# The hand-over from attention to routed experts: other places for five row stores, a list's steps and an early read

## The chip, the cores and the metric

The kernel runs on one core of a Trainium2 chip. The metric is the device time of one execution in microseconds. Shown are the median of three timed runs and one execution under the hardware profiler, from which all rows of the trace come.

The engines are named as in the profile: PE (TensorE), DVE (VectorE), ACT (ScalarE), POOL (GpSimd) and SP (SyncE, which here only issues transfers and loads registers). A transfer issued by SP or POOL runs on the core's DMA engines.

## The reference

Block-causal attention over 8 batches of 8 heads (576 positions, head size 64), whose output, transposed to 4608 rows of 512, goes through a mixture of experts with 4 groups of 4 experts; each row goes to the best expert of its best group.

```python
def _attn_ref(q, k, v):
    scores = np.matmul(q, k.transpose(0, 1, 3, 2)) / np.sqrt(D)
    scores = np.where(block_i >= block_j, scores, -1e9)      # blocks of 64
    attn = softmax(scores)
    return np.matmul(attn, v)

def _moe_ref(x, w_group, w_expert, w1, w2):                  # x: 4608 x 512
    g_idx = np.argmax(x @ w_group, axis=1)
    for g in range(4):
        xg = x[g_idx == g]
        e_idx = np.argmax(xg @ w_expert[g], axis=1)
        for e in range(4):
            h = np.maximum(xg[e_idx == e] @ w1[g, e], 0.0)   # 512 -> 1024
            ye = h @ w2[g, e]                                # 1024 -> 512
            out[rows of e] = (g_weight * e_weight)[:, None] * ye
```

## The kernel before, in words

**Attention.** The 64 heads are worked on in 32 pairs, one `period` for each; a pair is on the way over several periods. What an engine does in a period follows a list written by hand (`ORDER`): S are the scores, D the row maxima (L214), E the exponentials (L224), T the transposes of the weights (L252) with their copies t, V the values products (L291) with their copies v into the tile `xT`. Four pairs make a batch of 576 rows, and for each batch the router's tokens run in the same list: X0, X1, ... transpose `xT` back and store the scaled rows (`xns`) to the table of rows `xd` in memory; L, n, Y, M and G0 to G4 compute the router's logits, the choice and each row's place in its expert's list (`base` counts the rows of each expert); Z0 to Z4 scatter a batch's row numbers into the lists (`tab`), by POOL.

**The early list.** When five of the eight batches are counted, the fullest expert has its first 512 rows. `early` picks it with a few small DVE instructions and writes its number and the list's start to `rowe`. It is a generator: whoever calls `next` on it gets the instructions up to the next `yield`. The loop over pairs hangs such calls behind tokens of a period (`behind`; `eb` is 19, so `eb + 8` is period 27). SP then reads `rowe` into registers (`index`), reads the list from `tab` into `idse` (`getids`, L899) and loads the expert's weights, one piece for each `ask(1)` (`rawe`, 512 KB, L937). POOL gathers the 512 rows (`xge`, L910). So the first expert's two products (`g1`, L1009, and `g2`, L1059) can begin before the last batch is routed.

**The seam.** After the loop `seam` ends the attention of the last pair, and from then on PE runs the expert's plan (`moe.run`): g1 of piece 0, 1, 2, g2 of piece 0, g1 of 3, g2 of 1, and so on in turn. After place n of this plan come the calls in `moe.hooks[n]`: the last batch's router tokens (`last` is batch 7, `before` 6, `third` 5), the row stores X0 to X4 of the last batch (four PE transposes, eight ACT scalings at L648, one store at L649), and the four steps of `final`. `final` is a generator too: on DVE it computes from the counts the plan of all other lists, and its last step stores it to `rowi` (L558). Hook 6 also reads the first planned list (`getids` of slot 1: the registers from the plan by L880 and L881, then five reads of `tab` into `ids`, L899), and hook 7 gathers its rows from `xd` (`xg`, L910, by POOL). That gather reads rows of any batch, so it waits for every row store. PE transposes the gathered rows (L968). Behind each place the plan also splits weights into a high and a low half (`whe` by ACT at L953, `wle` by DVE at L954); L1032 on DVE makes the low half of a hidden piece (`hring`, `hx`), whose high half ACT makes at L1025.

Each engine, and each queue of transfers, works through its instructions in the order in which the program issues them.

```python
for h in hooks.get(n, []):       # moe.run: behind place n of the plan
    h()
```

Of the kernel before, what the change touches and what calls it, by code (L numbers as in the profile page):

```python
# [13 lines left out]
ALU = mybir.AluOpType  # L14
# [92 lines left out]
class Attention:  # L107
# [30 lines left out]
    def one(self):  # L138
        if self.after:
            return self.psT(), None  # L140
        h = self.banks.take(0, 1)
        return self.banks.view(h.ids[0]), h
# [237 lines left out]
class Router:  # L380
# [111 lines left out]
    def early(self, row):  # L492
        one = [R, 1]
        cnt = self.tt(self.base[0:R], self.eb, ALU.subtract)
        mx = self.red(cnt, ALU.max)
        sc = self.stt(cnt, mx[:, 0:1], self.edesc, ALU.is_ge, ALU.mult)
        m2 = self.red(sc, ALU.max)
        yield
        oh = self.ts(sc, m2[:, 0:1], ALU.is_equal)
        self.stt(cnt, 512.0, oh, ALU.min, ALU.mult, out=self.taken)  # L500
        self.ts(m2[0:1], -1.0, ALU.mult, float(NE), ALU.add, out=row[0:1, 0, 0:1])
        st = self.red(self.tt(oh, self.eb, ALU.mult))
        self.nc.vector.tensor_copy(row[0:1, 0, 1:2], st[0:1])
        yield

    def final(self, row):
# [309 lines left out]
def make_consts(tc, pool):  # L816
    nc = tc.nc
    ident = pool.tile([P, P], F32, name="ident")
    make_identity(nc, ident)
    return dict(ident=ident)  # L820
# [437 lines left out]
def seam(at, ro, moe, inner, ctx, N, rowi):  # L1258
    e, last, before, third = moe.slots[0], N // 4 - 1, N // 4 - 2, N // 4 - 3
    a = lambda i, *tok: at.token(i, tok, N)  # L1260
    r = lambda b, *toks: [ro.token(at, b, (t[0], int(t[1]))) for t in toks]
    at.on_dve = SEAM_DVE
    ro.later = set()
    y, z = N - 2, N - 1

    r(before, "X2", "X0", "X1")
    moe.advance(2, 99)
    at.gated()
    moe.gather(e, 3)
    r(third, "Z0")  # L1270
    a(y, "V", 0)
    a(y, "V", 1)
    a(y, "v", 0)
    moe.advance(2, 99)
    a(y, "v", 1)
    r(before, "G0", "G1", "G2")
    for g in (1, 0, 2):
        a(z, "T", g)
        a(z, "t", g, 0)
        a(z, "t", g, 1)  # L1280
    held = [at.banks.take(0, 1), at.banks.take(0, 1), at.banks.take(1, 2)]
    hold = [(0, 0), (1, 0), (2, 0), (2, 1)]
    for c, (n, m) in enumerate(hold):
        moe.xt_turn(e, c, at.banks.view(held[n].ids[m]))
    r(last, "R0")
    r(third, "Z1", "Z2")
    a(z, "V", 0)
    a(z, "V", 1)
    for c, (n, m) in enumerate(hold):
        moe.xt_split(e, c)  # L1290
        held[n].done()
    a(z, "v", 0)
    moe.advance(2, 99)
    a(z, "v", 1)
    inner.close()
    moe.open(ctx)
    moe.grow()
    moe.ngat = moe.nxt = len(e["ch"])
    at.after = at.moe = True
    fin = ro.final(rowi)  # L1300
    step = lambda: next(fin, None)
    one = lambda *toks: [lambda t=t: r(*t) for t in toks]
    moe.hooks = {
        0: one((last, "L0", "n0", "n1", "L1", "n2", "n3"), (before, "G4", "G3"), (third, "Z3", "Z4")),
        1: one((last, "Y0", "M0", "Y1", "M1", "Y2", "M2", "G0", "G1", "G2"), (before, "Z0", "Z1")),
        2: one((last, "X0"), (before, "Z2", "Z3")),
        3: one((before, "Z4"), (last, "X1")),
        4: one((last, "G4", "G3")) + [step],
        5: one((last, "Z0", "Z1", "Z2", "X2")) + [step] * 2,
        6: one((last, "Z3", "Z4", "X3")) + [step, lambda: moe.getids(moe.slots[1])],  # L1310
        7: one((last, "X4")) + [moe.hold, lambda: moe.gathers(1e9, True)],
    }
    at.spare = [(4, 5), (6, 7), (4, 5), (6, 7), (2, 3)]
    moe.steps = moe.run(moe.hooks)


@with_exitstack
def attention_moe(ctx, tc, q, k, v, wcat, w1, w2, out, order=None, on_dve=None):
    nc = tc.nc
    order = order or ORDER  # L1320
    on_dve = ON_DVE if on_dve is None else on_dve
    N = q.shape[0]
    NBAT = N // 4
    dp = ctx.enter_context(tc.tile_pool(name="dp", bufs=1, space=bass.MemoryType.DRAM))
    tab = dp.tile([TABR, TROW], I32, name="tab")
    xd = dp.tile([NTOK + 1, 512], F32, name="xd")
    cp = ctx.enter_context(tc.tile_pool(name="cp", bufs=1))
    consts = make_consts(tc, cp)
    rowe = cp.tile([1, 1, 2], I32, name="rowe")
    rowi = cp.tile([1, R, 2], I32, name="rowi")  # L1330
    rowo = cp.tile([1, R, 2], I32, name="rowo")
    cnti = cp.tile([1, 1], I32, name="cnti")
    inner = ExitStack()
    ET = mybir.EngineType
    with tc.manual_schedule(engines={ET.PE, ET.Activation, ET.DVE, ET.Pool, ET.SP}):
        ro = Router(tc, ctx, consts, wcat, tab, xd)
        moe = Moe(tc, ctx, consts, ro, w1, w2, out)
        at = Attention(tc, ctx, inner, q, k, v, consts)
        at.router, moe.at = ro, at
        warm = cp.tile([P, 1], F32, name="warm")  # L1340
        nc.vector.memset(warm, 0.0)
        nc.scalar.activation(warm, warm, AF.Exp)
        at.start(N, on_dve)
        at.clear()
        pre = ro.setup()
        eb = 4 * EBAT - 1
        slots = [moe.slot("e", FULL, rowe, slice(0, 1))]
        slots += [moe.slot(i, CAPS[i], rowi, slice(i, i + 1)) for i in EXEC]
        moe.plan(slots)
        ear = ro.early(rowe)  # L1350
        e = slots[0]
        for x in range(N):
            behind = {}
            if 2 <= x < 8:
                step = len(order) // HK
                behind = {order[step * z + step - 1][0]: [lambda: next(pre, None)] for z in range(HK)}
            if x == eb + 2:
                behind = {("T", 0): [lambda: moe.blank(e, 0), lambda: moe.blank(e, 1)]}
            if x == eb + 3:
                behind = {("T", 0): [lambda: moe.blank(e, 2), lambda: moe.blank(e, 3)]}  # L1360
            if x == eb + 8:
                behind = {t: [lambda: next(ear, None)] for t in (("S", 0), ("V", 1), ("T", 0))}
            if x in (eb + 9, eb + 10, eb + 11):
                behind = {("V", 1): [lambda: moe.index(e), lambda: moe.ask(1)]}
            if x == eb + 10:
                behind["end"] = [lambda: moe.getids(e)]
            if x == eb + 12:
                behind = {("V", 1): [lambda: at.load_v(N - 1), lambda: moe.ask(1)]}
            ahead = [lambda c=c: (at.gated(), moe.gather(e, c)) for c in {eb + 11: (0, 1), eb + 12: (2,)}.get(x, ())]
            at.period(x, N, order, behind, ahead)  # L1370
        seam(at, ro, moe, inner, ctx, N, rowi)
        spl = ro.spill(at, rowo, cnti)
        hooks = moe.hooks
        for n in range(60, 66):
            hooks[n] = [lambda: next(spl, None)]
        for _ in moe.steps:
            pass
    moe.overflow(cnti, rowo)
# [47 lines left out]
```

## Time and profile before

| | |
|---|---|
| median of three runs | 745.92 us (744.05 to 746.36) |
| the profiled execution's own time | 742.96 us |
| its span, first to last instruction | 741.2 us |
| what lies around the span | 1.8 us |
| PE, DVE, ACT, POOL busy | 97%, 63%, 60%, 35% of the span |
| bytes moved | 129.89 MB, 175 GB/s over the span |

Busy shares are means over stages with different limits. The attention and the experts differ, and the seam between them lies at about 262 to 330 us of the span. An idle engine costs something only where what it waits for ends last.

### The profile page before, as it was taken

What the parts mean: (1) busy time and instruction counts of PE and PEld (TensorE: products, weight loads), DVE (VectorE), ACT (ScalarE), POOL (GpSimd) and SP (SyncE); (2) the same over time, 40 slices, a digit from 0 to 9 for tenths busy, and PEclk for the clock granted to TensorE, in tenths of its full rate; (3) what the DMA queues carried; (4) which work ended last, traced back from release to release, by engine and by line L of the source; (5) the groups of instructions that cost most, each with busy time, mean ns of one, the idle gap of its engine ahead of it and who ended that gap; (6) DMA issues with size and microseconds to landing.
All of it is one profiled execution on the core that took longest, in us unless ns stands there. A gap on an engine that the chain in (4) does not pass through costs nothing.

```text
span 741.2 us, 20996 instructions
## 1 busy us (share of the span) xinstructions
PE 719.5 (97%) x7944; PEld 590.6 (80%) x7944; DVE 468.6 (63%) x1166; ACT 445.5 (60%) x1204; POOL 262.9 (35%) x560
## 2 busy tenths in 40 slices
PE   7999999999999999879999999999999999999996
PEld 4777777777777777769988888888898998888894
DVE  4878889888898877524335437537566456655642
ACT  6999898999989874424334335425455445544531
POOL 5534466665755654413121402302311303103102
PEclk9999999999999999989999999999999999999999
DMA  6953536264554642363335762672667428538441
GB/s 227 370 172 132 194 90 230 85 225 142 170 193 148 216 147 66 107 246 128 107 123 198 233 252 81 204 271 95 188 214 291 145 86 292 188 114 280 153 163 44
DMA packets 51623, 129.89 MB, mean 175 GB/s; under 512 B 12646, under 2 KB 13286, under 8 KB 51520
## 3 DMA queue, kind: packets, MB, share of 16 engines
q1 hardware_dynamic: 42592, 103.94, 41.6%
q0 software_dynamic: 8928, 24.60, 9.2%
q8 instruction: 63, 1.03, 0.6%
q14 instruction: 40, 0.33, 0.1%
HBM read 104.05 MB, written 24.59 MB: 174 GB/s over the span
## 4 chain that ended last, share of the span: by engine, by line
PE 87%; DVE 3%; ACT 3%; DMA 3%; issue 2%; POOL 1%; SPq 1%; POOLq 0%; DVEq 0%; ACTq 0%
PE psum L1059 23%; PE psum L1009 23%; PE psum L291 11%; PE psum L209 10%; PE psum L252 7%; PE psum L1004 5%; PE psum L1064 2%; PE psum L968 2%; ACT pb L224 2%; PE psum L1079 2%; DMA xd<-xns 1%; PE psum L658 1%; DMA xg<-xd,ids 1%; PE psum L301 1%; DMA idse<-tab 1%
## 5 line engine op out<-in xcount | busy, mean ns | idle before, releaser
L224 ACT ACTIVATE pb<-psum,nm 128x384 f32<-128x384 f32 (+8 forms) x288 | 149.6, 543 | 22.4 <-DVE nm L214 22.2
L1009 PE MATMUL psum<-xt,wh 128*128 128x264 f32 (+6 forms) x704 | 155.4, 312 | 0.0
L214 DVE TENSOR_REDUCE nm<-psum 128x1 f32<-128x384 f32 (+8 forms) x288 | 118.7, 482 | 13.8 <-PE psum L209 13.0
L1105 POOL DMA_INDIRECT out_dram<-ys,ids x40 | 41.0, 1025 | 238.9 <-DVE ys L1101 221.1
L1009 PEld LDWEIGHTS psum<-xt,wh 128*128 128x128 f32 x704 | 118.9, 188 | 8.1 <-issue 1.7
L1009 PE MATMUL psum<-xt,wl 128*128 128x264 f32 (+6 forms) x352 | 109.2, 310 | 0.0
L1025 ACT ACTIVATE hring<-psum 128x256 fp32r<-128x256 f32 (+5 forms) x68 | 32.0, 471 | 124.6 <-PE psum L1009 55.7
L1059 PE MATMUL psum<-wh,hring 128*128 128x512 f32 x306 | 106.6, 399 | 0.0
L291 PE MATMUL psum<-pt,vb 128*64 128x64 f32 (+4 forms) x1152 | 94.1, 317 | 0.6 <-ACT pt L268 0.6
L954 DVE TENSOR_TENSOR wl<-raw,wh 128x512 fp32r<-128x512 f32 x144 | 93.1, 686 | 1.7 <-ACT wh L953 1.5
L291 PEld LDWEIGHTS psum<-pt,vb 128*64 128x64 f32 x1152 | 66.5, 137 | 34.3 <-ACT pb L224 9.2
L209 PE MATMUL psum<-natk,natq 64*64 64x128 f32 (+5 forms) x1792 | 90.5, 339 | 2.8 <-ACT pb L224 1.2
L1032 DVE SCALAR_TENSOR_TENSOR hring<-psum,hring 128x256 fp32r<-128x256 f32 (+4 forms) x91 | 37.3, 431 | 81.7 <-ACT hring L1025 81.6
L268 ACT COPY pt<-psum 128x512 f32<-128x512 f32 x159 | 81.7, 619 | 1.5 <-PE psum L252 1.5
L953 ACT CAST wh<-raw 128x512 fp32r<-128x512 f32 x144 | 82.2, 620 | 0.2
L209 PEld LDWEIGHTS psum<-natk,natq 64*64 64x64 f32 x1792 | 57.4, 133 | 26.3 <-issue 3.4
L910 POOL DMA_INDIRECT xg<-xd,ids x40 | 40.8, 1020 | 85.7 <-PE psum L968 37.7
L1009 PEld LDWEIGHTS psum<-xt,wl 128*128 128x128 f32 x352 | 66.2, 188 | 1.0
L1059 PEld LDWEIGHTS psum<-wh,hring 128*128 128x128 f32 x306 | 57.5, 188 | 11.5
L224 ACT ACTIVATION_READ_ACCUMULATOR pb<-psum,nm 128x1 f32 x288 | 62.9, 218 | 0.0
L252 PE MATMUL psum<-ident,pb 64*128 64x64 f32 x1536 | 58.9, 225 | 2.9 <-ACT pb L224 2.6
L1059 PE MATMUL psum<-wl,hring 128*128 128x512 f32 x153 | 60.2, 393 | 0.0
(217 smaller groups left out, 1122.2 us busy)
## 6 DMA issues: line engine op xcount, KB each, us to landing
raw<-in_w_dram SPq DMA_DIRECT2D x72, 512.0 KB, 4.5
vb<-in_v_dram SPq DMA_DIRECT2D x32, 384.0 KB, 4.8
natk<-in_k_dram SPq DMA_DIRECT2D x32, 288.0 KB, 4.6
natq<-in_q_dram SPq DMA_DIRECT2D x32, 288.0 KB, 5.6
wh<-in_w_dram SPq DMA_DIRECT2D x16, 512.0 KB, 4.8
xd<-xns SPq DMA_DIRECT2D x14, 512.0 KB, 2.8
keep<-in_w_dram SPq DMA_DIRECT2D x12, 512.0 KB, 4.3
kept<-in_w_dram SPq DMA_DIRECT2D x12, 512.0 KB, 7.3
```

The source lines that it names most:

```text
L209: self.gate = nc.tensor.matmul(st[bank][c:c + 64, c0:c0 + n], lhsT=q[ps, BLK * t:BLK * t + BLK], rhs=k[ps, k0:k0 + n], start=True, stop=Tr ...
L214: self.nc.vector.tensor_reduce(out=r["nm"][:, t:t + 1], in_=r["s", t], op=ALU.max, axis=AX.X if t < 8 else AX.XY, negate=True)
L224: nc.scalar.activation(reg, r.pop(("s", t)), AF.Exp, bias=r["nm"][:, t:t + 1], accum_out=self.sms[b][:, pr, t:t + 1])
L252: self.gate = self.nc.tensor.transpose(out=out[a], in_=x[ps], identity=self.c["ident"][ps, ps], tile_position=(64 * a, 0))
L268: self.nc.scalar.copy(dst, src)
L291: nc.tensor.matmul(o[64 * a:64 * a + 64, BLK * (t0 - b0):BLK * (t1 - b0)], lhsT=r["v"][:, a, j, :], rhs=r["pt"][:, PHALF * (a ^ f) + c0:PH ...
L910: self.nc.gpsimd.indirect_dma_start(out=x[0:n], out_offset=None, in_=src, in_offset=bass.IndirectOffsetOnAxis(ap=s["ids"][0:n, c, 0:1], ax ...
L953: nc.scalar.copy(h[:, sl], s["raw", u][:, sl])
L954: nc.vector.tensor_tensor(out=l[:, sl], in0=s["raw", u][:, sl], in1=h[:, sl].bitcast(F32), op=ALU.subtract)
L1009: nc.tensor.matmul(o, lhsT=ww[:, dc, f], rhs=rr[:, dc, t], start=dc == 0 and x == 0, stop=dc == 3 and x == 2)
L1059: nc.tensor.matmul(y[c][0:n], lhsT=hh, rhs=w, start=k == 0 and x == 0, stop=k == 7 and x == 2)
L1105: i = nc.gpsimd.indirect_dma_start(out=self.out, out_offset=bass.IndirectOffsetOnAxis(ap=s["ids"][0:n, c, 0:1], axis=0), in_=ys[0:n], in_o ...
```

## The change

Three edits, all in the order of work; no computation is added or left out.

1. In `early` the `yield`s stand at other places: five pieces instead of two, and the product `taken`, which only `final` reads, comes last. The pieces hang behind tokens of two pairs (`eb + 8` and `eb + 9`) instead of one.
2. The registers of the early list are read at the end of period `eb + 9` instead of behind its V1; the list itself (`idse`) is read behind V1 of period `eb + 10`, ahead of that period's weight load, instead of at the period's end.
3. In the seam's hooks X0 comes in hook 0 (was 2), X1 in 2 (was 3), X2 in 3 (was 5), X3 in 4 (was 6), X4 in 5 (was 7). The steps of `final` are two in hook 4 and two in hook 5 (were one, two and one).

```diff
         cnt = self.tt(self.base[0:R], self.eb, ALU.subtract)
         mx = self.red(cnt, ALU.max)
+        yield
         sc = self.stt(cnt, mx[:, 0:1], self.edesc, ALU.is_ge, ALU.mult)
         m2 = self.red(sc, ALU.max)
         yield
         oh = self.ts(sc, m2[:, 0:1], ALU.is_equal)
-        self.stt(cnt, 512.0, oh, ALU.min, ALU.mult, out=self.taken)
         self.ts(m2[0:1], -1.0, ALU.mult, float(NE), ALU.add, out=row[0:1, 0, 0:1])
+        yield
         st = self.red(self.tt(oh, self.eb, ALU.mult))
         self.nc.vector.tensor_copy(row[0:1, 0, 1:2], st[0:1])
+        yield
+        self.stt(cnt, 512.0, oh, ALU.min, ALU.mult, out=self.taken)
         yield
...
-        0: one((last, "L0", "n0", "n1", "L1", "n2", "n3"), (before, "G4", "G3"), (third, "Z3", "Z4")),
+        0: one((last, "L0", "n0", "n1", "L1", "n2", "n3"), (before, "G4", "G3"), (last, "X0"), (third, "Z3", "Z4")),
         1: one((last, "Y0", "M0", "Y1", "M1", "Y2", "M2", "G0", "G1", "G2"), (before, "Z0", "Z1")),
-        2: one((last, "X0"), (before, "Z2", "Z3")),
-        3: one((before, "Z4"), (last, "X1")),
-        4: one((last, "G4", "G3")) + [step],
-        5: one((last, "Z0", "Z1", "Z2", "X2")) + [step] * 2,
-        6: one((last, "Z3", "Z4", "X3")) + [step, lambda: moe.getids(moe.slots[1])],
-        7: one((last, "X4")) + [moe.hold, lambda: moe.gathers(1e9, True)],
+        2: one((last, "X1"), (before, "Z2", "Z3")),
+        3: one((before, "Z4"), (last, "X2")),
+        4: one((last, "G4", "G3")) + [step] * 2 + one((last, "X3")),
+        5: one((last, "Z0", "Z1", "Z2")) + [step] * 2 + one((last, "X4")),
+        6: one((last, "Z3", "Z4")) + [lambda: moe.getids(moe.slots[1])],
+        7: [moe.hold, lambda: moe.gathers(1e9, True)],
...
-            if x == eb + 8:
+            if x in (eb + 8, eb + 9):
                 behind = {t: [lambda: next(ear, None)] for t in (("S", 0), ("V", 1), ("T", 0))}
-            if x in (eb + 9, eb + 10, eb + 11):
-                behind = {("V", 1): [lambda: moe.index(e), lambda: moe.ask(1)]}
+            if x == eb + 9:
+                behind["end"] = [lambda: moe.index(e), lambda: moe.ask(1)]
             if x == eb + 10:
-                behind["end"] = [lambda: moe.getids(e)]
+                behind = {("V", 1): [lambda: moe.getids(e), lambda: moe.ask(1)]}
+            if x == eb + 11:
+                behind = {("V", 1): [lambda: moe.ask(1)]}
```

The built programs show the new order. First SP's queue in the seam, from the fourth row store of the last batch (`xns_3`) to the first weight load of the first planned list; before, where the last row store (`xns_4`) stands behind the five reads of the list (`ids`):

```order
L649 DMA xd<-xns_3_6247 128x512
L558 DMA rowi<-fin_6267 1x64x2
L880 TENSOR_LOAD fin_6267
L881 TENSOR_LOAD fin_6267
L899 DMA ids_6289<-tab 128x4x2
L899 DMA ids_6289<-tab 16x2
L649 DMA xd<-xns_4_6317 64x512
L937 DMA raw_0_6338<-in_w_dram 128x1024
```

In the changed program (its lines have numbers three higher) the same instructions of SP stand so:

```order
L652 DMA xd<-xns_3_6191 128x512
L561 DMA rowi<-fin_6243 1x64x2
L652 DMA xd<-xns_4_6251 64x512
L883 TENSOR_LOAD fin_6243
L884 TENSOR_LOAD fin_6243
L902 DMA ids_6303<-tab 128x4x2
L902 DMA ids_6303<-tab 16x2
L940 DMA raw_0_6338<-in_w_dram 128x1024
```

The last row store has moved ahead of the register loads and the list's reads; of these the row of 16x2 stands for four.

Second, DVE at the end of `final`, from the last instructions of its third step (`fin`) on; before:

```order
L474 TENSOR_SCALAR fin_6217<-fin_6211 64x1
L954 TENSOR_TENSOR wle_6220<-rawe_5707,whe_6219 128x512 x2
L1032 SCALAR_TENSOR_TENSOR hring<-psum,hring 128x512
L484 SCALAR_TENSOR_TENSOR fin_6257<-fin_6209,pid,fin_6201 64x16
L484 SCALAR_TENSOR_TENSOR fin_6257<-scan_439,fin_6211,fin_6213 64x16
L474 TENSOR_SCALAR vals<-fin_6215,fin_6217 64x16
L479 TENSOR_TENSOR fin_6261<-vals,fin_6257 64x96
```

And DVE in the changed program:

```order
L474 TENSOR_SCALAR fin_6231<-fin_6225 64x1
L484 SCALAR_TENSOR_TENSOR fin_6233<-fin_6223,pid,fin_6183 64x16
L484 SCALAR_TENSOR_TENSOR fin_6233<-scan_439,fin_6225,fin_6227 64x16
L474 TENSOR_SCALAR vals<-fin_6229,fin_6231 64x16
L479 TENSOR_TENSOR fin_6237<-vals,fin_6233 64x96
L489 TENSOR_REDUCE fin_6239<-fin_6237 64x3
L474 TENSOR_SCALAR fin_6241<-fin_6239 64x1
L558 CAST fin_6243<-fin_6239 64x1
L479 TENSOR_TENSOR fin_6243<-fin_6239,fin_6241 64x1
L957 TENSOR_TENSOR wle_6262<-rawe_5707,whe_6261 128x512 x2
L1035 SCALAR_TENSOR_TENSOR hring<-psum,hring 128x512
```

The two weight splits and the low half of a hidden piece stand behind the fourth step instead of ahead of it.

Third, SP in period `eb + 10`, from the last pair's queries (`natq`) on; before:

```order
L170 DMA natq_5064<-in_q_dram 128x576
L937 DMA rawe_5152<-in_w_dram 128x1024
L638 DMA xd<-xns_2_5163 64x512
L638 DMA xd<-xns_0_5221 128x2x512
L638 DMA xd<-xns_1_5257 128x2x512
L899 DMA idse<-tab 128x4x2
```

And SP in the changed program:

```order
L170 DMA natq_5064<-in_q_dram 128x576
L902 DMA idse<-tab 128x4x2
L940 DMA rawe_5154<-in_w_dram 128x1024
L641 DMA xd<-xns_2_5165 64x512
L641 DMA xd<-xns_0_5223 128x2x512
L641 DMA xd<-xns_1_5259 128x2x512
```

The read of the early list now stands ahead of a weight load and three row stores.

## Rows read from the trace of the kernel before

**Rows 1.** The page: busy us of PE; the granted clock in 40 slices, in tenths.

```profile
PE 719.5 (97%) x7944; PEld 590.6 (80%) x7944; DVE 468.6 (63%) x1166; ACT 445.5 (60%) x1204; POOL 262.9 (35%) x560
...
PEclk9999999999999999989999999999999999999999
```

**Rows 2.** Waits, 262 to 330 us: who for whom, us in total, times, longest.

```profile
PE psum L968 <- DMA xg<-xd,ids: 6.9, 1, 6.9
```

**Rows 3.** Windows: length, PE, PEld, DVE, ACT, POOL busy, clock, DMA share, GB/s.

```profile
313.20:318.20 5.00, 0.00 (x0) 0.00 (x0) 0.00 (x0) 0.00 (x0) 3.78 (x5) 1.00 0.97 354
318.40:325.00 6.60, 4.96 (x14) 4.11 (x15) 1.89 (x3) 1.62 (x3) 0.42 (x2) 0.50 1.04 399
```

**Rows 4.** Chain that ended last, 240 to 410 us: start, us, what.

```profile
278.61 2.84 PE psum L1009 x12
...
301.14 1.20 DVE wle L954 x2
...
302.94 0.29 DVE fin L484 x2
...
304.33 0.49 SPq L558
...
306.78 0.41 SPq L899
...
309.38 2.29 DMA xd<-xns
...
312.53 7.46 DMA xg<-xd,ids
320.04 1.12 PE psum L968 x4
321.15 4.66 PE psum L1009 x12
...
373.09 0.44 PE psum L968 x4
```

**Rows 5.** DMA issues, 300 to 330 us: what, count, KB each, us to landing.

```profile
ids<-tab SPq DMA_DIRECT2D x1, 4.0 KB, 1.9
```

**Rows 6.** Timeline of ACT: start, us, what, count, idle before it.

```profile
281.47 0.60 ACT L1025 ACTIVATE hring<-psum 128x512 fp32r<-128x512 f32 x1 [2.60 <-PE psum L1009]
...
302.02 1.71 ACT L648 ACTIVATE xns<-psum,ri 64x64 f32<-64x64 f32 x8 [0.41 <-PE psum L643]
```

**Rows 7.** Timeline of PE in the seam.

```profile
307.37 0.62 PE L1009 MATMUL psum<-xte,whe 128*128 128x512 f32 x2
```

**Rows 8.** Timeline of SP's queue in the seam.

```profile
310.03 0.44 SPq L937 DMA_DIRECT2D raw<-in_w_dram  x1
```

**Rows 9.** Timeline of POOL, attention's end and the seam.

```profile
239.19 0.96 POOL L799 DMA_INDIRECT tab<-pay,pi  x1 [0.60 <-issue]
...
251.90 1.14 POOL L910 DMA_INDIRECT xge<-xd,idse  x1 [3.39 <-DMA idse<-tab]
...
301.82 1.31 POOL L799 DMA_INDIRECT tab<-pay,pi  x1 [0.22 <-issue]
```

**Rows 10.** Tile `tab`, 299 to 304 us: landing of its scatters.

```profile
DMA to landing us min/median/max: 2.4/2.4/2.4
```

**Rows 11.** Line L910, 245 to 270 us (early list's gathers): landing.

```profile
DMA to landing us min/median/max: 3.3/3.3/3.3
```

**Rows 12.** Timeline of PE, 215 to 272 us: where it was idle.

```profile
228.55 2.60 PE L209 MATMUL psum<-natk,natq 64*64 64x256 f32 x52 [0.43 <-DVE xT L264]
...
256.03 1.19 PE L209 MATMUL psum<-natk,natq 64*64 64x288 f32 x16 [0.47 <-DVE tmp L681]
...
261.36 1.21 PE L252 MATMUL psum<-ident,pb 64*128 64x64 f32 x32 [0.41 <-ACT pb L224]
```

**Rows 13.** Chain that ended last, attention's end.

```profile
242.39 2.54 DMA xd<-xns
...
247.18 3.89 DMA idse<-tab
```

## The prediction

> **What bounds the kernel now.** I began with the page: TensorE (PE) is busy 719.5 us, 97% of the span, so only its idle stretches can be won back [rows 1]. Measurement tells 0.3% (2.2 us) from no change. Next the waits by length around the hand-over from attention to experts: one stands out, PE idle 6.9 us before a transpose of `xg`, ended by the gather of the first planned list's rows [rows 2]. Then the windows across that hole: PE does nothing from 313.2 to 318.2 us, with the granted clock still 1.00, and in 318.4 to 325 us the clock is 0.50 (1.2 GHz), so PE works at half speed after the hole as well [rows 3]. Hence the hole is priced twice, and the second price is seen in the chain: 12 matmuls of L1009 take 4.66 us at 321.15, and 12 of the same line 2.84 us at 278.61; four transposes take 1.12 us, and later 0.44 us. Sum (4.66 - 2.84) + (1.12 - 0.44) = 2.5 us [rows 4].
>
> The chain also tells what the hole waits for [rows 4]: the last steps of `final` on VectorE (DVE) from 302.94, the list's store (`rowi`) at 304.33 on SyncE's queue (SP), the first index read at 306.78, then the last row store, X4, issued at 309.38 and landed 2.29 us later (311.67), the gather at 312.53, and PE at 320.04. PE had finished everything else at 320.04 - 6.89 = 313.15. The index read was ready earlier: it is a 4 KB read that lands in 1.9 us [rows 5], at 308.7. So the row store, which stands behind five index reads in SP's queue, ends last, by 3 us, though ScalarE (ACT) had scaled those rows by 302.02 + 1.71 = 303.7 [rows 6].
>
> **The change at the seam, part by part.**
> 1. X0 moves two hooks up. PE does its four transposes (0.44 us, by the same shape in rows 4) before L1009's second group instead of after the third. ACT scales X0 in a stretch in which it was idle for 2.6 us ahead of 281.47, so a scaling's 1.71 us cost nothing there [rows 6]. But the second group's hand-over, and behind it all of DVE's router work up to `final`, come later: +0.4 on the chain. X1 to X4 follow in the places that X0 to X3 left, or one earlier; ACT has as many of them ahead of `final` as before.
> 2. `final` runs two steps and two steps. Its last piece no longer stands behind two L954 and one L1032 on DVE: from 302.94 back to 301.14 is -1.8 us [rows 4]. Those three now come 1.8 us later, and the next pair with them, which PE wants first at 307.37 [rows 7]; the pair used to follow `final` directly, at 304.3, and takes another 1.2 us, so it is ready near 306 and hidden. Without that cover the price is at most the 1.8 us.
> 3. X4's store is issued right behind `rowi` and ahead of the index reads. It holds SP from 309.38 to the next issue at 310.03 [rows 8]: +0.65 for the reads. Its own landing (about 303.0 + 0.65 + 2.3 = 306) is ahead of theirs.
>
> The new index read is issued at 306.78 - 1.80 + 0.4 + 0.65 = 306.0, and lands 1.9 us later at 307.9. It also needs the last table scatter, which starts at 301.82 [rows 9] and lands in 2.4 us [rows 10], so at 304.6 with the 0.4: early enough. From the landing of what ended last to the gather was 312.53 - 311.67 = 0.86 us, so the gather starts at 308.8 instead of 312.5.
>
> How long the gather then takes no row settles, since six weight loads of 512 KB start at nearly the same time. From gather start to PE was 7.46 us [rows 4], with five of those loads issued ahead of it. The early list's gathers, 256 KB as well, landed in 3.3 us with fewer loads ahead [rows 11]. These are the bounds. Now the loads follow the index reads, which take 2.5 us to issue (306.78 to 309.28), so the first load goes out at about 308.6 and stands alone ahead of the gather. That is nearer the early list's case: I take 4.7 us. PE starts at 308.8 + 4.7 = 313.5, and what is left of the hole is 0.4 us (bounds 0 and 308.8 + 7.46 - 313.15 = 3.1 us). The idle stretches of up to 0.5 us in rows 12 were followed by no fall of the clock (the digit 9 throughout that part of rows 1), so I take the 2.5 us as won. Seam: 6.9 - 0.4 + 2.5 = 9.0 us.
>
> The Trainium skill (DMA: Bandwidth & Descriptors, section Queues, rings and completion order) says that each DMA engine takes turns between its queues, a packet at a time, whatever is still queued in one of them. By that rule the gather would land in about 3.3 us again, and the seam would give 9.4 us. The trace agrees in part only: 7.46 us behind five loads is more than taking turns explains.
>
> **The early list, costed apart.** Seven small DVE instructions stood between two copies of `xT`; two stay, five go elsewhere. PE waited 0.43 us for the second copy at 228.55 [rows 12]. DVE has the same sum of work, now beside other waits. Bounds 0 and 0.43; I take 0.3, since PE's wait ended on that copy alone.
> The read of `idse` used to be issued at 247.18, behind three row stores, and landed 3.89 us later [rows 13]; POOL stood 3.39 us waiting for it [rows 9], and with it the router's partial sums, on which DVE, ACT and PE waited in turn: PE 0.47 us at 256.03 and 0.41 at 261.36 [rows 12], together 0.88. Now it is issued as soon as the last scatter of the fifth batch lands: 239.19 [rows 9] and 2.4 [rows 10], 241.6; so POOL's wait goes. But SP stands at that read, and behind it come the second weight load (512 KB) and the three row stores. The first of these was issued at 242.39 and landed in 2.54 us [rows 13]; the third store's buffer waits for that landing. With the load's 0.52 MB ahead of it, at 354 GB/s [rows 3], it lands 1.5 us later, and DVE with it. So this part lies between -1.5 and +0.88; I take 0, nearer the gain's end than the middle, since DVE had slack in its wait on POOL.
> The list's end comes some 4 us later on DVE. The loads queued behind it on SP belong to a pair one period away: nothing.
>
> **Sum.** 9.0 + 0.3 + 0 = 9.3 us off the profiled execution's own 742.96 us: 733.7 us. That execution was 3.0 us below the median of the three runs, so taken off the median of 745.92: **736.6 us**. Its own range: most 6.9 + 2.5 + 0.43 + 0.88 = 10.7 (735.2 us), least 6.9 - 3.1 + 2.5 - 1.5 = 4.8 (741.1 us).
>
> **Rivals.**
> - *The hole moves to the next parts.* PE needs the second and third parts of the list at 313.5 + 0.44 + 2.84 = 316.8. Were packets served in the order of issue, six loads and three gather parts (3.1 + 0.8 MB from 308.6 on, at 354 GB/s) would take 11 us, to 319.6. PE would wait some 3 us there and the clock might fall again (2.5 us). Gain 9.3 - 3 = 6.3 or, with the clock, 3.8: 739.6 to 742.1 us. For it: the loads keep the DMA engines full in both windows of rows 3 (share 0.97 and 1.04). Against it: before, with more loads ahead, PE waited for a gather once only [rows 2]. Chance 0.12.
> - *The row store does not hold the gather.* If the chain names the wrong one and the gather waits for the index reads, only 1.8 - 0.4 = 1.4 us come forward, and 0.65 is lost again to X4's place: 0.8 us, 745.1, no change. Against it: the gather's start follows X4's landing by 0.86 us, and the first read's by 3.8. Chance 0.05.
> - *The early read blocks SP (slower).* SP waits at `idse` in the middle of attention with row stores and a value load behind it. Were the scatter to land late, every microsecond would go to the third row store's buffer, to DVE and to PE. It decides once the stores go out later than 242.4 by more than the seam's 9.0 us: at 253.6, with 2.2 us more, the kernel is 2.2 us slower, 748.1. Against it: the scatter lands at 241.6, before the store was issued. Chance 0.03.
>
> **How the numbers follow.** My forecast has 0.80, the rivals 0.12, 0.05 and 0.03. Faster by over 0.3%: 0.80 and nearly all of 0.12, so 0.91; the same 0.06; slower 0.03. The range runs from 734.0 us (the most, less 1.2 us, half the spread of the runs, 744.05 to 746.36) to 741.5 us: it takes in the least gain and most of the first rival.
>
> **What would show it.** Right: PE's idle before `xg` under 1 us; no window at clock 0.50 in that part; in SP's row X4's store between `rowi` and the index reads; the gather starting near 308.8, less what the early list gave; POOL without its 3.39 us before `xge`. Wrong: a wait of 2 us or more on `xg` that remains, or comes at the second or third part, with the clock at 0.50; DVE standing at the third row store near 245 us for more than 2 us; the chain going through L954 at 307 us.

## The result, and the profile after

| | before | changed |
|---|---|---|
| median, same chip | 745.40 us (744.05 to 746.36, 4 runs) | 737.32 us (736.17 to 738.50, 4 runs) |
| profiled execution, own time | 742.96 us | 736.96 us |
| span | 741.2 us | 735.1 us |

The ratio is 0.9903, 95% interval 0.9886 to 0.992 (the quotient of the two medians is 0.9892, inside it). The medians differ by 8.1 us, the two profiled spans by 6.1 us. The profile shows where the 6.1 us came from, and also that more was won and some lost again.

SP's queue in the seam (start, us, what, count):

```profile
302.55 0.49 SPq L561 DMA_DIRECT2D rowi<-fin  x1
303.13 0.55 SPq L652 DMA_DIRECT2D xd<-xns  x1
305.78 3.45 SPq L902 DMA_DIRECT2D ids<-tab  x5
309.42 0.35 SPq L940 DMA_DIRECT2D raw<-in_w_dram  x1
```

POOL, the first gather of the first planned list:

```profile
308.51 1.01 POOL L913 DMA_INDIRECT xg<-xd,ids  x1 [5.78 <-DMA ids<-tab]
```

and the landing of these gathers in the view of that line, which has it for three of the five (the second, fourth and fifth) and not for the first:

```profile
DMA to landing us min/median/max: 5.8/6.2/6.6
```

The row store stands ahead of the reads, and the gather waits for the index read now. It starts at 308.5 instead of 312.5 [rows 4]. It also starts ahead of the first weight load (309.42), where before it stood behind five, and its bytes came sooner for it. The DMA queues, with packets, MB and share of the 16 engines; q0 carries POOL's gathers, q1 what SP issues. Changed kernel, 310.00 to 312.50 us, where the gather's 0.26 MB move:

```profile
q0 software_dynamic: 80, 0.26, 56.6%
q1 hardware_dynamic: 86, 0.34, 32.7%
```

Kernel before, 313.80 to 317.00 us, behind the end of POOL's first gather instruction (312.53 + 1.26); q0 has no row, its bytes begin behind 317.0:

```profile
q1 hardware_dynamic: 300, 1.09, 96.2%
```

The chain that ended last (start, us, what):

```profile
292.43 1.82 ACT xns L651 x8
294.29 0.66 PE psum L646 x4
294.95 4.34 PE psum L1062 x12
...
302.51 2.81 PE psum L1062 x12
...
316.45 0.44 PE psum L971 x4
316.89 2.81 PE psum L1012 x12
```

The chain no longer passes through a gather: PE works without a pause up to the first transposes of `xg`. They start at 316.45 instead of 320.04, 3.59 us sooner, and these four transposes and the 12 products behind them take 0.44 and 2.81 us where they took 1.12 and 4.66 [rows 4], 2.53 us less. Together 6.12 us, which is the whole of the span's gain.

But PE reaches that point 3.3 us later than its own work allowed before (316.45 against 320.04 - 6.89 = 313.15). The first rows of the chain say why. X3's transposes wait for a PSUM bank that ScalarE was still reading for X2; the row of PE in the timeline, with the idle time ahead of it in brackets:

```profile
294.29 0.66 PE L646 MATMUL psum<-ident,xT 128*128 128x128 f32 x4 [1.84 <-ACT xns L651]
```

The 12 products behind them take 4.34 us and not 2.8: the granted clock stands at 0.50, the lower of the two levels (1.2 GHz), behind that pause. Windows (length, PE busy, clock, DMA share, GB/s):

```profile
295.60:299.00 3.40, 3.40 (x10) 0.50 0.28 104
299.00:305.00 6.00, 6.00 (x30) 1.00 0.13 27
```

1.84 + (4.34 - 2.80) = 3.4 us, the 3.3 us that are missing.

In the early list's part three waits of PE [rows 12] are gone, 0.43 + 0.47 + 0.41 = 1.31 us, and one is new. PE's timeline there, then the piece of the chain that it hangs on, then POOL's gather for the early list:

```profile
246.74 2.55 PE L209 MATMUL psum<-natk,natq 64*64 64x320 f32 x40 [1.39 <-DVE xns L636]
```

```profile
241.87 4.00 DMA xd<-xns
245.99 0.70 DVE xns L636
```

```profile
250.22 1.14 POOL L913 DMA_INDIRECT xge<-xd,idse  x1 [0.77 <-issue]
```

The first of the three row stores now lands in 4.00 us instead of 2.54 [rows 13], because the second weight load goes out just ahead of it (an experiment below shows this), and DVE, then PE, wait for the buffer. POOL's 3.39 us [rows 9] have shrunk to 0.77.

### The profile page after: what moved, and what is told of

It reads as the page before. It is cut to its first block, busy times and chain, and to the rows that moved or that the text cites. A ratio compares the mean times of both kernels' runs of the same rounds, so it can differ in the third digit from the quotient of the medians.

```text
span 735.1 us, 20992 instructions
## 1 busy us (share of the span) xinstructions
PE 718.7 (98%) x7944; PEld 590.2 (80%) x7944; DVE 468.0 (64%) x1166; ACT 445.3 (61%) x1204; POOL 261.2 (36%) x560
## 4 chain that ended last, share of the span: by engine, by line
PE 91%; ACT 2%; DVE 2%; POOL 2%; DMA 1%; issue 1%; POOLq 0%; DVEq 0%; ACTq 0%
PE psum L1062 25%; PE psum L1012 23%; PE psum L291 11%; PE psum L209 11%; PE psum L252 8%; PE psum L1007 5%; PE psum L1067 3%; PE psum L971 2%; PE psum L1082 2%; ACT pb L224 1%; DMA xd<-xns 1%; PE psum L661 1%; PE psum L301 1%; POOL tab L802 1%; DVE nm L214 0%
```

## The experiments

They were run in three sets, each on a chip of its own, with the kernel before run beside them: medians of before 749.6 us (first set), 749.7 (second) and 749.3 (third). Ratios are to these; absolute times are compared inside a set only.

**First set: which part carries the gain.** The seam's hooks alone, with the early list as before, its pieces too:

```diff
-            if x in (eb + 8, eb + 9):
+            if x == eb + 8:
...
+            if x == eb + 10:
+                behind["end"] = [lambda: moe.getids(e)]
```

> The kernel before with the new hooks of the seam alone; the early list as before. My theory: nearly all of the gain is the seam's, and the early list's two halves (a wait of PE gone at 228 us, a new one of 1.4 us at 246 us) nearly cancel. Then this runs within 0.5 us of the changed kernel, some 8 us under the kernel before; PE waits 1.8 us for X3's transposes, with a stretch at 1.2 GHz behind it, and not at all for xg. Rival: the early list carries 2 us or more of the gain, and this is 739 us or more.

The early list's edits alone, with the seam's hooks as before:

```diff
-        0: one((last, "L0", "n0", "n1", "L1", "n2", "n3"), (before, "G4", "G3"), (last, "X0"), (third, "Z3", "Z4")),
+        0: one((last, "L0", "n0", "n1", "L1", "n2", "n3"), (before, "G4", "G3"), (third, "Z3", "Z4")),
...
+        4: one((last, "G4", "G3")) + [step],
...
+        7: one((last, "X4")) + [moe.hold, lambda: moe.gathers(1e9, True)],
```

> The early list's new pieces and read alone; the seam's hooks as before. My theory: 0.3 us under the kernel before, no more than can be told from no change; PE idle 0.0 at 228 us (was 0.43), 1.4 us at 246 us (was none), none at 256 and 261 us (were 0.47 and 0.41); the hole of 6.9 us before xg and the half clock behind it as in the kernel before. Rival: a gain of 2 us or more, if the list's read frees more than the store behind it costs; or a loss of 1.5 us, if the late store costs more than PE's 1.4 us.

Measured: the seam alone 742.13 us, ratio 0.9909 (0.989 to 0.9927); the early list alone 749.22 us, ratio 0.9989 (0.9975 to 1.0004). So the seam is nearly the whole gain, and the early list gives nothing that can be measured. PE's rows, seam alone:

```profile
299.86 0.66 PE L643 MATMUL psum<-ident,xT 128*128 128x128 f32 x4 [1.85 <-ACT xns L648]
324.45 0.63 PE L968 MATMUL psum<-ident,xg 128*128 128x128 f32 x4 [0.33 <-DMA xg<-xd,ids]
```

and early list alone:

```profile
252.23 4.18 PE L209 MATMUL psum<-natk,natq 64*64 64x320 f32 x40 [1.92 <-DVE xns L636]
...
328.67 1.12 PE L971 MATMUL psum<-ident,xg 128*128 128x128 f32 x4 [7.76 <-DMA xg<-xd,ids]
```

Each part carries its own new stall: X3's bank comes with the hooks, the row store's with the early read. With the early list alone the hole stands as before. Two details were not as expected: with the seam alone no stretch at 1.2 GHz follows X3's wait, and a wait of 0.33 us for `xg` is left. The early list's profile is that of its slowest execution (752.71 us); in it the 40 products behind the new stall take 4.18 us, where they take 2.55 us in the changed kernel.

**The two new stalls.** X3 and X4 one hook later, X4 still ahead of the index reads:

```diff
-        4: one((last, "G4", "G3")) + [step] * 2 + one((last, "X3")),
-        5: one((last, "Z0", "Z1", "Z2")) + [step] * 2 + one((last, "X4")),
-        6: one((last, "Z3", "Z4")) + [lambda: moe.getids(moe.slots[1])],
+        4: one((last, "G4", "G3")) + [step] * 2,
+        5: one((last, "Z0", "Z1", "Z2")) + [step] * 2 + one((last, "X3")),
+        6: one((last, "Z3", "Z4", "X4")) + [lambda: moe.getids(moe.slots[1])],
```

> The changed kernel with X3 in hook 5 and X4 in hook 6, one place later each. My theory: X3's transposes waited 1.84 us because two PSUM banks take turns for X1, G4, X2 and X3, and ACT was still scaling X2 out of the bank that X3 gets; the half clock that followed cost another 1.5 us. One place later the bank is free: no wait at 294 us, no stretch at clock 0.50 there, PE is done with its own work 3.5 us sooner and then waits 0 to 1.5 us for the second and third part of xg. Total 733.8 to 735.5 us, 2 to 3.5 under the changed kernel. Rival: the wait is of ACT being late with whatever comes there, or the clock falls for another reason; then the wait or the 0.50 stretch stays and the time is that of the changed kernel, 737 us.

The second weight load behind the three row stores instead of ahead:

```diff
-                behind = {("V", 1): [lambda: moe.getids(e), lambda: moe.ask(1)]}
+                behind = {("V", 1): [lambda: moe.getids(e)], "end": [lambda: moe.ask(1)]}
```

> The changed kernel with the second weight load of the early list moved from right behind the read of idse to the end of that period, behind the three row stores. My theory: the first row store landed 4.0 us after its issue (2.5 before) since the load's 512 KB stood ahead of it; without it it lands in 2.5 us again, DVE's wait for the third store's buffer is 0.5 to 0.7 us instead of 2.17, PE's 1.39 us at 246.7 us shrinks to 0.3 or less, and the total falls by 0.8 to 1.5 us to about 736 us. Rival: the store lands late because the read of idse goes out in front of it; then the landing and the 1.39 us stay.

Measured, same set: 742.00 us, 0.9898 (0.9878 to 0.9919), and 741.37 us, 0.9898 (0.9878 to 0.9918). Neither can be told from the seam alone, nor from the changed kernel's 0.9903, so the gains that were expected (2 to 3.5 us and 0.8 to 1.5 us) did not show. The causes of the two stalls are confirmed all the same, since each edit removed the stall that it was aimed at and no other: with the load behind, PE does not wait near 246 us at all, and X3's wait stays:

```profile
296.99 0.66 PE L646 MATMUL psum<-ident,xT 128*128 128x128 f32 x4 [1.83 <-ACT xns L651]
```

With X3 later its wait is gone, and PE stands further on instead:

```profile
321.13 0.66 PE L971 MATMUL psum<-ident,xg 128*128 128x128 f32 x4 [1.73 <-DMA xg<-xd,ids]
...
325.78 0.63 PE L971 MATMUL psum<-ident,xg 128*128 128x128 f32 x4 [0.75 <-DMA xg<-xd,ids]
```

2.5 us, in two pieces. X3's stall had hidden the end of the gathers in part; take it away and they end last again. The other part is their place among the loads: here SP issues the first load at 315.52, 0.06 us ahead of the gather's start, and two loads' bytes go first. The queues from 316.60 to 319.50, then from 319.50 to 321.00 us:

```profile
q1 hardware_dynamic: 266, 1.02, 92.8%
...
q1 hardware_dynamic: 65, 0.20, 54.6%
q0 software_dynamic: 80, 0.26, 47.8%
```

**Second set: both stalls out, and the steps of the chain one by one.** Both edits above together:

> The changed kernel with X3 and X4 one place later in the seam and the early list's second weight load behind the row stores. Theory (two small stalls of the changed kernel, independent of each other): no PE wait for X3's bank near 295 us and none of 1.39 us near 246 us; what is left is a PE wait for the gathered rows of about 2.5 us in two pieces, as when only X3 was moved. The early stall's 1.4 us stays gained, so the ratio to the kernel before is about 0.988, some 1.3 us under the kernel with X3 moved alone. Rival: time taken out of the early part comes back in a later wait, and the ratio stays at 0.9898.

On top of X3 and X4 later, the last row store behind the index reads:

```diff
-        6: one((last, "Z3", "Z4", "X4")) + [lambda: moe.getids(moe.slots[1])],
+        6: one((last, "Z3", "Z4")) + [lambda: moe.getids(moe.slots[1])] + one((last, "X4")),
```

> X3 one place later, and the last row store X4 issued behind the reads of the index instead of ahead of them. Theory of the prediction (the gather waits for the later of row store and index read): the gather's start is now set by the row store, which is issued about 2.5 us later than the first index read and lands some 2 us behind its issue, so the gather starts about 2 us later, its wait in the profile is put down to the store, the PE waits for gathered rows grow from 2.5 to about 4.5 us, and the ratio rises from 0.9898 to about 0.9925. Rival (the row store does not hold the gather): the index read comes 0.5 us sooner and the gather with it, the PE waits are 2 to 2.5 us, and the ratio is 0.989 to 0.990.

Or the list's steps in three places:

```diff
-        4: one((last, "G4", "G3")) + [step] * 2,
+        4: one((last, "G4", "G3")) + [step],
...
-        6: one((last, "Z3", "Z4", "X4")) + [lambda: moe.getids(moe.slots[1])],
+        6: one((last, "Z3", "Z4")) + [step] + one((last, "X4")) + [lambda: moe.getids(moe.slots[1])],
```

> X3 one place later, and the steps of the last list in three places (1, 2, 1) instead of two (2, 2), which is nearer to the kernel before. Theory of the prediction (the list's end sets the index read and the gather): the list's last step ends 1 to 2 us later, and so do the index read and the gather; PE waits for gathered rows of 3.5 to 4.5 us instead of 2.5, ratio about 0.992. Rival: the steps' places do not matter, because VectorE has idle time there; gather at the same distance from the seam's start, waits of 2.5 us and a ratio of 0.9898.

Both stalls out: 742.89 us, ratio 0.9923 (0.9904 to 0.9941), so the expected 0.988 was missed. PE waits 2.56 and 0.27 us for `xg`, so what X3's edit wins is eaten there. That the early stall's time comes back in these waits, as the rival had it, is not shown: they are only 0.35 us longer than with X3 alone moved (2.83 against 2.48). The early stall's 1.4 us is too little to be told from nothing between two sets.

The store behind the reads: 750.75 us, ratio 1.0025 (1.0013 to 1.0036). One store, moved behind five small reads, undoes the change. SP, POOL and PE of that run:

```profile
315.93 2.50 SPq L902 DMA_DIRECT2D ids<-tab  x5
318.52 0.46 SPq L652 DMA_DIRECT2D xd<-xns  x1
319.17 0.44 SPq L940 DMA_DIRECT2D raw<-in_w_dram  x1
...
321.66 1.01 POOL L913 DMA_INDIRECT xg<-xd,ids  x1 [10.18 <-DMA xd<-xns]
...
329.12 1.11 PE L971 MATMUL psum<-ident,xg 128*128 128x128 f32 x4 [7.55 <-DMA xg<-xd,ids]
```

The gather's wait is put down to the store, as in the kernel before, and it starts 5.7 us behind the reads' issue instead of 2.7 (312.84 to 315.58 with X3 later). The rival that the store holds nothing is out. The list's store went out late in this run as well, 312.62 - 277.79 = 34.8 us behind the start of the last values product against 309.05 - 275.82 = 33.2 with X3 later; why, the trace does not tell. The expected hole of 4.5 us was too small for another reason too: a gather that starts 2.5 us behind the first weight load also takes longer, 321.66 to 329.12 = 7.5 us, against 321.13 - 315.58 = 5.5 us where it starts with the first load. So the wait for the first part grew from 1.73 to 7.55 us by about 3.0 for the store, 1.9 for the landing and 1.1 for the later list, less 0.2 by which PE itself was later. Behind the hole the clock is 0.60 over 6.4 us.

Steps 1, 2, 1: 746.95 us, ratio 0.9969 (0.9952 to 0.9985). The gather starts 317.88 - 276.43 = 41.45 us behind the last values product's start, against 315.58 - 275.82 = 39.76 with 2 and 2: 1.7 us later, for the 1.8 us of the prediction. PE's wait before the transposes of `xg` grows from 2.48 to 4.33 us (the trace names no releaser for it; from the gather's start to PE it is 6.6 us here). Behind it the clock is 0.62 in a window of 4 us, which by that share costs about 1.5 us more, and the ratio is above the expected 0.992.

**What holds the gather's landing.** Both stalls out, and the first planned list's weight loads wait for the second gather's landing; only the first of them carries the wait, the others stand behind it in SP's queue:

```diff
+HELD = 1
...
+        s["gi", c0] = self.nc.gpsimd.indirect_dma_start(
...
+        i = self.nc.sync.dma_start(raw.rearrange("p (c f) -> p c f", c=n), src)
+        if s.get("o") == 1 and ("gi", HELD) in s and not s.get("held"):
+            info = mybir.DependencyInfo(mybir.DependencyClass.Sync, mybir.DependencyReason.DATA)
+            self.tc.add_manual_dep(i.ins, s["gi", HELD].ins.name, info, reason="behind the gather")
+            s["held"] = True
```

> As the kernel with both stalls taken out, and the weight loads of the first list after the seam wait until the second chunk's gather has landed. Theory (the gather's landing of 5.8 to 6.6 us is the queue of 512 KB weight loads behind it, which share the DMA engines): the first two gathers land 3 to 4 us after their start, the PE waits for gathered rows fall from 2.5 us to 0.5 us or less, and the time is about 2 us under the kernel with both stalls out (ratio about 0.985 to 0.986). The weights come about 4 us later; their first cast was 10 us ahead of its product, so nothing waits for them. Rival 1: the landing is the gather's own time, the waits stay at 2.5 us and the ratio is that of the kernel with both out. Rival 2: the weights come too late and PE waits for them near 333 us or behind, as long as the gathers gained, or longer.

Measured: 744.19 us, ratio 0.9937 (0.9918 to 0.9956), no gain over both stalls out (0.9923). Yet half of the theory held: the first gather starts at 313.30 and PE transposes its rows at 316.95 without a wait, so it had landed in 3.65 us or less. The second rival took it back, by a way that I had not named. ACT and PE:

```profile
323.32 1.14 ACT L963 CAST wh<-raw 128x512 fp32r<-128x512 f32 x2 [5.15 <-DMA raw<-in_w_dram]
324.36 0.59 ACT L1035 ACTIVATE hring<-psum 128x512 fp32r<-128x512 f32 x1
324.85 1.06 ACT L994 CAST xt<-psum 128x512 fp32r<-128x512 f32 x2
...
326.52 1.65 PE L978 MATMUL psum<-ident,xg 128*128 128x128 f32 x8 [2.53 <-DVE xt L995]
```

The weights were not late for their product. But the cast of the first load stands in ACT's queue ahead of the copies of the gathered rows: ACT stood 5.15 us for the load, and the copies behind it came late. DVE, whose split of the same weights stands ahead of its own half of the copies, stood as long for that cast:

```profile
323.97 1.29 DVE L964 TENSOR_TENSOR wl<-raw,wh 128x512 fp32r<-128x512 f32 x2 [5.07 <-ACT wh L963]
```

PE waited 2.53 us, and over the next 6.40 us the clock was 0.51.

**Third set: only the second load waits**, so that the cast has its weights:

```diff
-        if s.get("o") == 1 and ("gi", HELD) in s and not s.get("held"):
+        if s.get("o") == 1 and u > 0 and ("gi", HELD) in s and not s.get("held"):
```

> As the kernel whose loads are held, but the first of the weight loads goes at once, and only the second and all behind it wait for the second chunk's gather. With all loads held the gathers landed in time, but ScalarE's first cast of the weights stood 5.15 us in its queue waiting for the first load, ahead of the copies of the gathered rows, and TensorE stood 2.53 us for those copies and then ran 6.4 us at half clock. Theory: the first cast comes on time again, one load beside the gathers costs them no more than its own 1.3 us, TensorE waits under 1 us in all for gathered rows or their copies, and the ratio is 0.003 under that of the kernel with all held or with none held (0.9937 and 0.9923 measured), about 0.990. Rival: any load beside the gathers holds them as long as the whole queue did, and the waits for gathered rows stay at 2.5 us, ratio 0.992.

> The changed kernel itself, on the chip of the experiments. Ratio 0.990 as in the first comparison if the chip makes no difference to the change. In the experiments' profiles ScalarE and VectorE stood 2.6 us longer before the copies of the last logits' second half than in the first profile of the changed kernel; if that belongs to the chip or the day, this profile shows it too; if it belongs to the edits, it does not.

> The kernel before itself, for its profile on the chip of the experiments. If the 2.6 us wait ahead of the last logits' copies belongs to the chip or the day, it stands here too, and the hole ahead of the gathered rows is longer than the 6.9 us of the first profile (about 8 us); if not, neither.

The second load held: **739.55 us, ratio 0.9866 (0.9846 to 0.9885)**, against 743.60 us, 0.9923 (0.9905 to 0.9941), for the changed kernel on the same chip. It beats both kernels, and by more than expected (0.990). Both stalls out without a held load gave 0.9923 (0.9904 to 0.9941) in the second set; the intervals do not overlap, so the two moves alone do not explain the gain. SP, and PE at the transposes of `xg`:

```profile
314.40 0.35 SPq L943 DMA_DIRECT2D raw<-in_w_dram  x1
319.75 0.35 SPq L943 DMA_DIRECT2D keep<-in_w_dram  x1
...
318.50 0.66 PE L978 MATMUL psum<-ident,xg 128*128 128x128 f32 x4 [0.23 <-issue]
```

The second load goes out 5.4 us behind the first. The gather starts at 314.57 and has landed by 318.50, in 3.9 us or less beside one load. PE does not wait for it or for a copy. Its span is 4.1 us shorter than that of the changed kernel in this set (742.1 to 738.0), which is the sum of the waits of PE that it lacks: X3's 1.86, the gather's 0.85, and 1.41 of the 1.80 us at the early row store. The changed kernel's three:

```profile
251.62 2.55 PE L209 MATMUL psum<-natk,natq 64*64 64x320 f32 x40 [1.80 <-DVE xns L636]
...
301.19 0.66 PE L646 MATMUL psum<-ident,xT 128*128 128x128 f32 x4 [1.86 <-ACT xns L651]
326.31 0.63 PE L971 MATMUL psum<-ident,xg 128*128 128x128 f32 x4 [0.85 <-DMA xg<-xd,ids]
```

and the early one where the second load is held:

```profile
250.07 2.55 PE L211 MATMUL psum<-natk,natq 64*64 64x320 f32 x40 [0.39 <-DVE xns L638]
```

The two kernels themselves, in profiles of this set: spans 747.2 and 742.1 us. ACT at the copies of the last logits, changed kernel:

```profile
282.98 0.37 ACT L268 COPY lt<-psum 128x256 f32<-128x256 f32 x1 [0.19 <-PE psum L661]
285.92 0.43 ACT L268 COPY lt<-psum 128x320 f32<-128x320 f32 x1 [2.57 <-remote]
```

kernel before:

```profile
285.89 0.43 ACT L268 COPY lt<-psum 128x320 f32<-128x320 f32 x1 [3.26 <-PE psum L1009]
...
325.80 1.11 PE L968 MATMUL psum<-ident,xg 128*128 128x128 f32 x4 [7.39 <-DMA xg<-xd,ids]
```

Both have a wait of 2.6 us or more there; in the first profiles of both kernels it was 0.17 us. So it is not the edits' doing. The hole was 7.39 us here (about 8 was expected), and 0.85 us is left of it in the changed kernel.

## Why the prediction held, and where its steps failed

736.6 us was predicted and 737.3 measured. The steps:

- **The hole and its clock: right.** PE does not wait for `xg` in the first profile of the changed kernel (0.85 us in the second), and the 2.5 us behind the hole are won (2.53).
- **What holds the gather: right, and shown twice.** The row store behind the reads brings the hole back (7.55 us, of which some 3 us are the store's own), and steps in three places delay the gather by 1.7 us (1.8 predicted). The gather's start was predicted at 308.8 and was 308.5; the difference is the index read, issued at 305.78 instead of 306.0.
- **"X1 to X4 follow in the places that X0 to X3 left, or one earlier", at nothing: the step that failed.** I counted ACT's scalings and not the banks that they read. In the program the transposes of these rows and G4's products take turns between two banks. Before, G4 stood between X1 and X2, and X3 got the bank that G4 had used. Now X2 stands ahead of G4, X3 gets X2's bank, and it came 1.84 us before ACT had read that bank out. With the clock at 0.50 behind it the price was 3.4 us in that profile. X3 one hook later removes it, as shown. "No window at clock 0.50 in that part" was therefore wrong. The stall also covered later waits for `xg`.
- **Gather to PE in 4.7 us: no wait came, but not for the reasons given.** The lower bound was misread: the 3.3 us [rows 11] are the landing of one gather of the early list, that at 258.40, and in 258.4 to 262.0 us the loads' queue moved nothing. So it is the landing of a gather alone, and not of one "with fewer loads ahead". The order came out the other way too: the first load was to go out ahead of the gather, at 308.6, but the five reads took 3.45 us to issue and not 2.50, and it went out at 309.42, behind the gather's start. The gather's bytes then began first (310.0, the load's 311.3) and were through by 312.5, 4.0 us behind its start. Where the first load goes out 0.03 to 0.12 us ahead of the gather, with the others close behind, 4.7 us was too little: 5.5 us (X3 later), 5.6 us (both stalls out) and 6.6 us or less (steps in three places). PE's waits of 2.5 and 2.8 us there are mostly for the first part; the first rival had put 3 us at the next parts, and 0.75, 0.27 and, in the changed kernel's second profile, 0.85 us came there. With the loads held back the first gather takes at most 3.65 us. The Trainium skill (DMA: Bandwidth & Descriptors, section Queues, rings and completion order) has each DMA engine take turns between its queues, from which the prediction took a landing of about 3.3 us. The trace does not agree at a gather's start: loads that are queued ahead move 1.02 MB (X3 later), or 1.09 MB and more (before), while the gathers' queue moves nothing. Behind that the two queues do share: 0.48 MB of gathers beside 0.71 MB of loads in 317.00 to 320.00 us of the kernel before.
- **The early list at 0.3 + 0: right in sum.** 1.31 us of waits gone, 1.39 us new; alone it measured 0.9989. The 1.5 us by which the row store was to land later was 4.00 - 2.54 = 1.46 us. I had put it beside DVE's slack; there was none, and PE paid nearly all of it.
- **From the profiled execution to the median.** 9.3 us off the profiled execution's own time was too much: it was 6.0. The median fell by 8.1, since the profiled execution of before lay 2.4 us under its median of these runs, and that of the changed kernel only 0.4. So the closeness of 736.6 is partly luck: two misses, one of 3.3 us inside the profile, about what X3's stall cost there, and one of some 2 us between profile and median, point opposite ways. That the gather got ahead of the first load was luck as well.

The rival in which the early read blocks SP did not come about: the read goes out at 240.84, and the row stores follow at 241.87, earlier than before.

## What to carry to other kernels

A producer's work that is moved forward needs its buffers and banks free at the new place as well as its inputs: look up who reads the bank that it will write, not only whether the engine is idle. A small urgent transfer did not overtake large ones that were queued ahead of it on another queue: issue it first, or hold the large ones back until it has landed, but let the first one go whose data an engine will wait for with other work queued behind. And when a wait is removed, price the next one behind it on the same engine; here taking out X3's stall showed nothing in the time until the gathers were helped too.

## What the runs showed of the hardware that was not expected

- The same stall does not always cost the clock. Behind X3's wait of 1.83 to 1.86 us the granted clock stood at 0.50 for 3.4 us in the first profile of the changed kernel (0.57 over as long with the load behind), and stayed at 1.00 with the seam alone and in the changed kernel's second profile (301.2 to 306 us). The waits are equal to 0.03 us. It is the same at the early row store: 0.59 and 0.60 over some 4 us behind waits of 1.92 us (early list alone) and 1.83 us (store behind the reads), and 1.00 behind 1.80 us in the changed kernel's second profile. And with both stalls out PE's 2.56 us before `xg` were followed by 1.00 over 3.9 us. What decides was not found.
- In the profiles of the three later sets ACT's copy of the second half of the last logits waits 2.6 us or more, mostly for no releaser that the trace names; in the first profiles of both kernels it waits 0.17 us. In the changed kernel the scaling of X0 then comes late, PE waits about 1 us for its bank, and the list's store goes out 33.2 us behind the start of the last values product instead of 31.6 (309.45 - 276.28, against 302.55 - 270.97). The median of before is 4 us higher on those chips too. Whether the chip is the cause, and by what, stays open.
- Loads on SP's queue kept a gather on POOL's queue waiting for its first byte. In the kernel before the gather had been issued by 313.79, and q0 moved nothing until 317.0; with no load ahead (all loads held) its bytes began at about 315.0, behind an issue that ended at 314.31. Why the loads go first is not shown.
